# Three late chunk loads of a recurrent-attention and MoE kernel issued in other forms

## The chip, the cores and the metric

The kernel runs on one core of one Trainium2 chip. The metric is the device time of one execution in microseconds (us). TensorE is called PE here, its weight loads PEld, VectorE DVE, ScalarE ACT, GpSimd POOL, SyncE SP. SP does no arithmetic: it issues DMA transfers. A "granted clock" of 1.00 means TensorE ran at full speed.

## The reference: what is computed

Two layers follow each other. The first is a recurrent attention (RWKV-6) over 4 batch rows, 8 heads, 768 positions and 48 values per head. Cut to what matters:

```python
for t in range(S):
    cur = einsum('bhd,bhe->bhde', u[None] * kt, vt)
    y[:, :, t] = einsum('bhd,bhde->bhe', rt, state + cur)
    state = wt[:, :, :, None] * state + einsum('bhd,bhe->bhde', kt, vt)
```

The second takes the result as 3072 tokens of 384 values through two matrix products with a leaky ReLU between them:

```python
h = x @ w_in                      # 384 -> 2048
g = np.maximum(0.01 * h, h)
return (g @ w_out)                # 2048 -> 384
```

Inputs `r`, `k`, `v`, `w` are `(4, 8, 768, 48)` float32 in DRAM, so one head's 128 positions are 24 KB that lie in one piece, and the eight heads lie 147 KB apart.

## The kernel before, in words

The 3072 tokens are cut into 24 chunks of 128 positions. `seq` says which batch row and which part of it chunk `n` is; the chunks interleave the batch rows. The first four chunks go through `pair`, two at a time, the others through `single(n)`. Each chunk of `single` has four loads (`w`, `k`, `r`, `v`, 192 KB each, line 708): 128 partitions by 8 heads by 48 floats, that is 1024 rows of 192 bytes into one buffer of the pool `in`, which holds the four parts side by side. A row of heads fills 1536 bytes of a partition without a gap.

From the loads, `single` makes these steps:

- ACT takes the logarithm of `w` (line 718), PE sums it along the positions (line 724), DVE adds (line 736), ACT takes exponentials (lines 750 and 754), DVE multiplies them with `r` and `k` into `rk` (helper line 407).
- `rk` is transposed into `rkT`: by PE for some chunks, by a DMA transpose from SP for the chunks in `RK_DMA` (line 771). PE forms the scores from `rkT` (line 864), DVE masks them into `m` (line 795).
- POOL multiplies `k` by `u` into `ru` (line 437) and that by `r` (line 441); DVE sums it per head into `dg` (line 445); POOL multiplies `v` by `dg` into `vs` (line 449), and casts `v` to bf16 into `vb` (line 457). POOL also scales the state into `sb` (line 782).
- PE makes `y` from `m`, `vb` and `sb` (lines 831 and 836), DVE adds `vs` (line 482), and `y` is transposed into `xT`, by PE (line 468) or by a DMA transpose from SP (line 849).

The second layer runs in blocks of one or two chunks: products with `w_in_b` (line 1030), leaky ReLU on ACT (line 1045), and, for the late blocks, products with `w_out_b` by a scheme of seven products (line 960) with sums on DVE (lines 941, 974, 981) and ACT (line 976). Line 1013 stores the result.

The order of all steps is written out by hand in `ORDER`, a list of 1123 step numbers, and each engine runs its own steps in that order and never passes one that waits. `Plan` keeps costs too, from which it picks a free buffer of a pool and places warm-up products at the start. The step numbers and `ORDER` are the same before and after the change.

Each DMA signals its landing on one of eight semaphores, `DMAHW0` to `DMAHW7`, which are handed out in turn. A DMA is issued only when the one before it on the same semaphore, eight places earlier, has landed. So at most eight DMAs are under way.

The change touches the function `load` in `single`, for the chunks 20, 21 and 22 of 0 to 23, whose buffers are `in6`, `in4` and `in8`. Chunks 20 and 21 run together (20 is in `MERGED`).

Of the kernel before, what the change touches and what calls it, by code (L numbers as in the profile page):

```python
# [7 lines left out]
F32 = mybir.dt.float32  # L8
# [159 lines left out]
def kernel(  # L168
# [11 lines left out]
    nc = tc.nc  # L180
    B, H, S, D = r.shape
    L = 128
# [36 lines left out]
    pool = ctx.enter_context(tc.tile_pool(name="pool", bufs=1))  # L219
# [3 lines left out]
    def make(name, count, shape, dtype, where=None):  # L223
        pools[name] = [(where or pool).tile(shape, dtype, name=f"{name}{i}") for i in range(count)]
# [12 lines left out]
    w_in_b = pool.tile([128, KT, FF], BF16, name="w_in_b")  # L237
    w_out_b = pool.tile([128, NJ, DM], BF16, name="w_out_b")

    make("in", 11, [128, 1536], F32)  # L240
    make("lw", 3, [128, H, 64], BF16)
    make("lw2", 1, [128, 2, H, 64], BF16)
# [17 lines left out]
    with tc.manual_schedule():  # L260
# [10 lines left out]
        for t in pools["lw"]:  # L271
# [3 lines left out]
            out=trev[:], in_=trev[:], compare_op=ALU.is_ge, fill=0.0,  # L275
# [5 lines left out]
            out=tstr2[:], in_=tstr2[:], compare_op=ALU.is_gt, fill=0.0,  # L281
# [4 lines left out]
            out=ident[:], in_=ident[:], compare_op=ALU.is_equal, fill=0.0,  # L286
# [3 lines left out]
            out=maskb[:], in_=maskb[:], compare_op=ALU.is_gt, fill=0.0,  # L290
            base=0, pattern=[[1, 128]], channel_multiplier=-1,
        )
        for tile_, op in ((mask2, ALU.is_gt), (spread, ALU.is_equal)):
            for q in (0, 64):
                nc.gpsimd.affine_select(
                    out=tile_[q : q + 64, :, :], in_=tile_[q : q + 64, :, :], compare_op=op, fill=0.0,
# [58 lines left out]
        def columns(n):  # L355
            xb, off = place[n]
            return lambda: xb.t[:, :, off : off + L]
# [23 lines left out]
        for part in (1, 2):  # L381
            def rest(e, part=part):
# [8 lines left out]
                out=u_rows.t[0:1, :], in_=u_row.t[0:1, :]),  # L391
# [302 lines left out]
        def single(n):  # L694
            b, c = seq[n]
            t0 = c * L
# [5 lines left out]
            def part(i):  # L702
                return lambda: slot.t[:, i * DM : (i + 1) * DM].rearrange("p (h d) -> p h d", h=H)

            lds = []
            for i, src in enumerate((w, k, r, v)):
                def load(e, src=src, i=i):
                    nc.sync.dma_start(out=part(i)(), in_=src[b, :, t0 : t0 + L, :].rearrange("h p d -> p h d"))
                lds.append(step(
                    {"SP": 0.62}, load, P0 + i * 0.1, takes=[slot], wire=LOAD,  # L710
                    deps=[firsts[n - AHEAD]] if n - AHEAD in firsts else []))
            wl, kl, rl, vl = lds
            wv, kv, rv, vv = (part(i) for i in range(4))

            lw = Buf("lw")
            s_ln = lns[n] = step(
# [24 lines left out]
            for half in range(0 if first else 2):  # L741
# [4 lines left out]
                        out=a_in.t[q0 : q0 + 64, :, half], in_=cp.t[q0 : q0 + 64, DM : DM + NP], func=AF.Exp),  # L746
# [21 lines left out]
            else:  # L768
# [3 lines left out]
                        out=rkT.t[:], in_=rk.t[:].rearrange("p a h d -> p (a h d)")),  # L772
# [4 lines left out]
            if not first:  # L777
# [5 lines left out]
                        out=sb.t[:].rearrange("p g a d -> p (g a) d"),  # L783
# [12 lines left out]
                    out=m.t[:, par, :, :], in0=sc[par].t[:].rearrange("p (g t) -> p g t", g=NP),  # L796
# [49 lines left out]
            else:  # L846
# [3 lines left out]
                        out=columns(n)(), in_=y.t[:].rearrange("p h d -> p (h d)")),  # L850
# [4 lines left out]
        def run(ns):  # L855
            works = [single(n) for n in ns]
            asked = [next(x) for x in works]

            def scores(e):
                for sc, rkT, _ in asked:  # L860
                    for p in range(NP):
                        for par in range(2):
                            q0 = 64 * par
                            nc.tensor.matmul(  # L864
                                sc[par].t[:, p * 128 : (p + 1) * 128], lhsT=rkT.t[q0 : q0 + D, NP + p, :],
                                rhs=rkT.t[q0 : q0 + D, p, :], start=True, stop=True, skip_group_check=True)

            s_sc = step(
                {"PE": 0.19 + 0.231 * len(ns)}, scores, ns[-1] * 10 + 1, deps=[s for x in asked for s in x[2]],
                reads=[x[1] for x in asked], takes=[b for x in asked for b in x[0]])  # L870
            given.append(s_sc)
            for x in works:
                next(x, None)
# [142 lines left out]
        for nb, size in enumerate(blocks):  # L1016
# [7 lines left out]
            for j in range(0, NJ, J):  # L1024
# [15 lines left out]
                if j == 0:  # L1040
                    for ch in chs:
# [4 lines left out]
                        out=g.t[:, j : j + J, 0:N],  # L1046
                        in_=hp.t[:, 0 : J * N].rearrange("p (a n) -> p a n", a=J), func=AF.Prelu, alpha=0.01),
# [86 lines left out]
```

## Time and profile before

| | |
|---|---|
| time, median of 3 runs | 179.33 us (179.13 to 180.84) |
| span of the profiled execution | 177.0 us |
| what lies around the span, against the median | 2.3 us |
| granted clock from 100 us to 160 us | 1.00 |
| PE busy | 170.4 us, 96% |
| DVE busy | 143.5 us, 81% |
| ACT busy | 114.0 us, 64% |
| POOL busy | 107.3 us, 61% |
| chunk loads from line 708 | 80, of 192 KB, 4.1 to 4.7 us from issue to landing |

The profiled execution has no time of its own beside its span, so the span stands for it: the difference to the median, 2.3 us, is taken as what every execution has before and after it. Rows of the timeline give the start (us from the span's start), the duration (us), the engine, the line, the operation, the tiles as out<-in, and how many instructions are merged in the row; a bracket tells how long the engine had been idle before and what ended that. A queue's row (SPq) is the time that the issuing of a DMA took, not its transfer. An answer about one line gives durations as minimum, median and maximum, and the time from issue to landing in the same way.

### The profile page before, as it was taken

Reading aid. Unit: us, or ns where it says so; the run is one execution under the profiler, and the core shown is the slowest. Engines: PE = TensorE matmul, PEld = TensorE weight load, DVE = VectorE, ACT = ScalarE, POOL = GpSimd, SP = SyncE. Lnnn points to the kernel's source line nnn. Section 1 sums busy time; section 2 is a strip of 40 time slices with the busy share of each in tenths; the row PEclk is TensorE's granted clock in tenths of the full one; section 3 lists DMA queues with packets and bytes.
Section 4 is the critical chain, followed back from the end, with each engine's and each line's share of the span. In section 5 each row is a group of like instructions: output and inputs, shape, how many; then the busy total and the mean of one; then the engine's idle time right before and its main releaser. Section 6 shows DMA issues by size and latency. Waiting matters only on the chain.

```text
span 177.0 us, 5530 instructions
## 1 busy us (share of the span) xinstructions
PE 170.4 (96%) x2155; PEld 139.9 (79%) x2158; DVE 143.5 (81%) x299; ACT 114.0 (64%) x263; POOL 107.3 (61%) x143
## 2 busy tenths in 40 slices
PE   7999999999999999999999999999999998999993
PEld 2566779867768877777779899899899997799992
DVE  7498935267599899889879999999999999956662
ACT  5676769734677794796379964676769950178500
POOL 5989946486749859879599093391693959100000
PEclk9999999999999999999999999999999999999999
DMA  5999999999999999999999999996999897432104
GB/s 138 261 271 340 350 300 195 351 231 199 201 206 195 191 199 227 163 201 179 198 206 195 197 208 209 163 222 124 210 194 196 188 226 78 118 101 80 44 26 157
DMA packets 115885, 34.25 MB, mean 194 GB/s; under 512 B 108305, under 2 KB 115090, under 8 KB 115858
## 3 DMA queue, kind: packets, MB, share of 16 engines
q1 hardware_dynamic: 115856, 33.89, 93.1%
q8 instruction: 17, 0.28, 0.7%
q14 instruction: 10, 0.08, 0.2%
q10 hardware_dynamic: 2, 0.00, 0.0%
HBM read 25.17 MB, written 4.72 MB: 169 GB/s over the span
## 4 chain that ended last, share of the span: by engine, by line
PE 69%; DVE 15%; ACT 5%; issue 4%; DMA 3%; POOL 2%; DVEq 0%; SPq 0%; ACTq 0%
PE ps L1030 30%; PE ps L1060 13%; PE ps L960 10%; DVE rk L407 3%; DMA rkT<-rk 3%; PE ps L864 3%; DVE in L941 2%; PE ps L418 2%; ACT g L425 2%; PE ps L724 1%; PE ps L836 1%; DVE ci L736 1%; PE ps L518 1%; DVE dg L445 1%; ACT ps L750 1%
## 5 line engine op out<-in xcount | busy, mean ns | idle before, releaser
L1030 PE MATMUL ps<-xT,w_in_b 128*128 128x256 bf16 (+1 forms) x672 | 70.8, 258 | 0.3 <-DVE rk L407 0.2
L1045 ACT ACTIVATE g<-ps 128x512 bf16<-128x512 f32 x96 | 54.4, 598 | 18.1 <-PE ps L1030 16.0
L1030 PEld LDWEIGHTS <-w_in_b 128*128 128x128 bf16 x672 | 56.9, 98 | 7.8 <-issue 0.6
L437 POOL TENSOR_TENSOR ru<-in,ub 128x384 f32<-128x384 f32 x24 | 24.3, 1017 | 13.1 <-DMA in<-in_k_dram 7.0
L1060 PE MATMUL ps<-w_out_b,g 128*128 128x384 bf16 x160 | 31.4, 326 | 0.0
L407 DVE TENSOR_TENSOR rk<-in,ps 128x384 bf16<-128x384 f32 x48 | 24.8, 547 | 6.1 <-ACT ps L754 2.3
L782 POOL TENSOR_TENSOR sb<-s,a 128x384 bf16<-128x384 f32 x18 | 15.6, 875 | 16.6 <-ACT a L745 8.1
L795 DVE TENSOR_TENSOR m<-ps,maskb 128x512 bf16<-128x512 f32 x40 | 25.1, 682 | 0.3 <-PE ps L864 0.2
L441 POOL TENSOR_TENSOR ru<-ru,in 128x384 f32<-128x384 f32 x24 | 23.8, 1000 | 2.1 <-DMA in<-in_r_dram 1.1
L1060 PEld LDWEIGHTS <-g 128*128 128x128 bf16 x160 | 14.1, 97 | 6.8
L449 POOL TENSOR_TENSOR vs<-in,dg 128x384 f32<-128x384 f32 x20 | 17.4, 874 | 3.0 <-DMA in<-in_v_dram 2.1
L960 PEld LDWEIGHTS <-g 128*128 128x128 bf16 x224 | 18.3, 98 | 0.2
L976 ACT COPY o<-ps 128x192 f32<-128x192 f32 x18 | 5.8, 320 | 17.5 <-PE ps L960 15.5
L960 PEld LDWEIGHTS <-in 128*128 128x128 bf16 x168 | 13.6, 98 | 1.9 <-DVE in L941 1.4
L445 DVE TENSOR_REDUCE dg<-ru 128x8 f32<-128x384 f32 x24 | 12.9, 545 | 1.9 <-POOL ru L441 1.7
L457 POOL CAST vb<-in 128x384 bf16<-128x384 f32 x24 | 12.7, 534 | 2.2 <-DMA in<-in_v_dram 2.2
L981 DVE TENSOR_TENSOR o<-ps,o 128x192 f32<-128x192 f32 x35 | 11.6, 351 | 1.9 <-ACT o L976 1.1
L482 DVE TENSOR_TENSOR y<-ps,vs 128x384 bf16<-128x384 f32 x20 | 10.9, 553 | 2.4 <-PE ps L836 2.3
L754 ACT ACTIVATE ps<-ci 128x384 f32<-128x384 f32 x20 | 9.8, 493 | 4.7 <-DVE ci L736 4.1
L718 ACT ACTIVATE lw<-in 128x384 bf16<-128x384 f32 x20 | 9.9, 521 | 4.1 <-DMA in<-in_w_dram 4.1
L736 DVE TENSOR_TENSOR ci<-ps,lw 128x384 f32<-128x384 f32 x20 | 10.9, 551 | 1.8 <-PE ps L724 1.1
L960 PE MATMUL ps<-in,in 128*128 128x192 bf16 x112 | 11.4, 247 | 0.5 <-DVE in L941 0.5
(105 smaller groups left out, 258.8 us busy)
## 6 DMA issues: line engine op xcount, KB each, us to landing
out_dram<-o SPq DMA_DIRECT2D x23, 192.0 KB, 2.8
in<-in_w_dram SPq DMA_DIRECT2D x20, 192.0 KB, 4.7
in<-in_k_dram SPq DMA_DIRECT2D x20, 192.0 KB, 4.2
in<-in_r_dram SPq DMA_DIRECT2D x20, 192.0 KB, 4.2
in<-in_v_dram SPq DMA_DIRECT2D x20, 192.0 KB, 4.1
in<-in_moe_w_out_dram SPq DMA_DIRECT2D x4, 768.0 KB, 6.9
in<-in_moe_w_in_dram SPq DMA_DIRECT2D x2, 768.0 KB, 9.7
in<-in_moe_w_in_dram SPq DMA_DIRECT2D x4, 384.0 KB, 8.1
```

The costliest lines, as they stand in the source:

```text
L407: (nc.gpsimd if e == "POOL" else nc.vector).tensor_tensor(out=o, in0=x, in1=i, op=ALU.mult)
L437: lambda e: nc.gpsimd.tensor_tensor(out=ru.t[:], in0=kv(), in1=ubv, op=ALU.mult),
L441: lambda e: nc.gpsimd.tensor_tensor(out=ru.t[:], in0=ru.t[:], in1=rv(), op=ALU.mult),
L445: lambda e: nc.vector.tensor_reduce(out=dg.t[:], in_=ru.t[:], axis=AX.X, op=ALU.add),
L449: lambda e: nc.gpsimd.tensor_tensor(out=vs.t[:], in0=vv(), in1=dg.t[:].unsqueeze(2).to_broadcast([128, H, D]), op=ALU.mult),
L457: {"POOL": 0.56}, lambda e: nc.gpsimd.tensor_copy(out=vb.t[:], in_=vv()),
L782: lambda e: nc.gpsimd.tensor_tensor(out=sb.t[:].rearrange("p g a d -> p (g a) d"), in0=s_in.t[:].rearrange("p g a d -> p (g a) d"), in1=a_ ...
L795: lambda e, par=par: nc.vector.tensor_tensor(out=m.t[:, par, :, :], in0=sc[par].t[:].rearrange("p (g t) -> p g t", g=NP), in1=maskb[:].uns ...
L960: nc.tensor.matmul(o(), lhsT=x()[:, i, :], rhs=y()[:, i, :], start=fresh, stop=(stop and i == ii[-1]), skip_group_check=True)
L1030: nc.tensor.matmul(hp.t[:, a * N : (a + 1) * N], lhsT=w_in_b[:, t, (j + a) * 128 : (j + a + 1) * 128], rhs=xb.t[:, t, 0:N], start=(a == 0 ...
L1045: lambda e, hp=hp, g=g, j=j, J=J, N=N: nc.scalar.activation(out=g.t[:, j : j + J, 0:N], in_=hp.t[:, 0 : J * N].rearrange("p (a n) -> p a n ...
L1060: nc.tensor.matmul(op.t[:, 0:DM], lhsT=g.t[:, j, off : off + 128], rhs=w_out_b[:, j, :], start=(j == 0), stop=(j == NJ - 1))
```

## The change

For chunk 20 the loads of `w` and `k` are each issued as eight transfers, one per head, of 128 rows of 192 bytes. For chunk 21 the load of `w` goes into a buffer of its own, `spaced`, in which the heads lie 64 floats (256 bytes) apart, and the logarithm reads it from there. For chunk 22 the load of `v` is issued by ACT instead of SP. The bytes that are moved are the same.

```diff
+    spaced = pool.tile([128, H, 64], F32, name="spaced")
     make("in", 11, [128, 1536], F32)
...
                 def load(e, src=src, i=i):
-                    nc.sync.dma_start(out=part(i)(), in_=src[b, :, t0 : t0 + L, :].rearrange("h p d -> p h d"))
+                    if n == 20 and i < 2:
+                        for h in range(H):
+                            nc.sync.dma_start(out=part(i)()[:, h], in_=src[b, h, t0 : t0 + L, :])
+                    elif n == 21 and i == 0:
+                        nc.sync.dma_start(
+                            out=spaced[:, :, 0:D], in_=src[b, :, t0 : t0 + L, :].rearrange("h p d -> p h d"))
+                    else:
+                        (nc.scalar if n == 22 and i == 3 else nc.sync).dma_start(
+                            out=part(i)(), in_=src[b, :, t0 : t0 + L, :].rearrange("h p d -> p h d"))
...
             wv, kv, rv, vv = (part(i) for i in range(4))
+            if n == 21:
+                wv = lambda: spaced[:, :, 0:D]
```

In the built program the lines shift: the loads of line 708 stand in lines 711 (per head), 713 (spaced) and 716 (all others), 771 becomes 782, 849 becomes 860, 1013 becomes 1024, 437 becomes 438, 441 becomes 442. Names carry a number for the buffer and a second one that is one higher after the change, since `spaced` came in as number 74.

**SP's queue, late in the program.** Before the change, from chunk 21's load of `w` to chunk 20's load of `r`:

```order
L708 DMA in4_78<-in_w_dram 128x8x48
L708 DMA in6_80<-in_w_dram 128x8x48
L1013 DMA out_0_dram<-o2_148 128x384
L849 DMA_TRANSPOSE xT4_144<-y0_132 128x3x128
L849 DMA_TRANSPOSE xT4_144<-y1_133 128x3x128
L771 DMA_TRANSPOSE rkT2_99<-rk3_95 128x8x128
L771 DMA_TRANSPOSE rkT3_100<-rk2_94 128x8x128
L708 DMA in6_80<-in_k_dram 128x8x48
L708 DMA in6_80<-in_r_dram 128x8x48
```

After it, at the same place ("x8" are eight rows in a run):

```order
L713 DMA spaced_74<-in_w_dram 128x8x48
L711 DMA in6_81<-in_w_dram 128x48 x8
L1024 DMA out_0_dram<-o2_149 128x384
L860 DMA_TRANSPOSE xT4_145<-y0_133 128x3x128
L860 DMA_TRANSPOSE xT4_145<-y1_134 128x3x128
L782 DMA_TRANSPOSE rkT2_100<-rk3_96 128x8x128
L782 DMA_TRANSPOSE rkT3_101<-rk2_95 128x8x128
L711 DMA in6_81<-in_k_dram 128x48 x8
L716 DMA in6_81<-in_r_dram 128x8x48
```

The order is the same; two rows became sixteen. The first group after the change, with the semaphores that each row waits for:

```order
L713 DMA spaced_74<-in_w_dram 128x8x48 [waits DMAHW3_49]
L711 DMA in6_81<-in_w_dram 128x48 [waits DMAHW4_49]
L711 DMA in6_81<-in_w_dram 128x48 [waits DMAHW5_49]
L711 DMA in6_81<-in_w_dram 128x48 [waits DMAHW6_49]
L711 DMA in6_81<-in_w_dram 128x48 [waits DMAHW7_49]
L711 DMA in6_81<-in_w_dram 128x48 [waits DMAHW0_49]
L711 DMA in6_81<-in_w_dram 128x48 [waits DMAHW1_49]
L711 DMA in6_81<-in_w_dram 128x48 [waits DMAHW2_49]
L711 DMA in6_81<-in_w_dram 128x48 [waits DMAHW3_49]
L1024 DMA out_0_dram<-o2_149 128x384 [waits DMAHW4_49,DVE_49]
```

The eighth head's transfer waits for `DMAHW3`, on which chunk 21's `w` (the first row) was issued.

**POOL, where chunk 20's `k` and `r` are used.** Before:

```order
L782 TENSOR_TENSOR sb1_129<-s1_123,a1_120 128x384 [waits DVE_49,Activation_49]
L437 TENSOR_TENSOR ru0_107<-in6_80,ub_70 128x384 [waits DMAHW2_49,Pool_49]
L441 TENSOR_TENSOR ru0_107<-ru0_107,in6_80 128x384 [waits DMAHW3_49,Pool_49]
L457 CAST vb1_102<-in10_84 128x384 [waits DMAHW4_49]
L449 TENSOR_TENSOR vs2_114<-in10_84,dg0_109 128x384 [waits DVE_49]
```

After:

```order
L793 TENSOR_TENSOR sb1_130<-s1_124,a1_121 128x384 [waits DVE_49,Activation_49]
L438 TENSOR_TENSOR ru0_108<-in6_81,ub_70 128x384 [waits DMAHW4_49,DMAHW3_49,DMAHW5_49,DMAHW2_49,DMAHW6_49,DMAHW1_49,DMAHW7_49,DMAHW0_49,Pool_49]
L442 TENSOR_TENSOR ru0_108<-ru0_108,in6_81 128x384 [waits DMAHW1_49,Pool_49]
L458 CAST vb1_103<-in10_85 128x384 [waits DMAHW2_49]
L450 TENSOR_TENSOR vs2_115<-in10_85,dg0_110 128x384 [waits DVE_49]
```

The order is the same; the first use of `k` waits for all eight of its transfers.

**ACT, where chunk 22's `v` is issued.** Before, in the run of `COPY`s of line 976:

```order
L976 COPY o1_147<-ps1_152 128x192 [waits PE_49]
L754 ACTIVATE ps4_155<-ci1_90 128x384
L976 COPY o2_148<-ps0_151 128x192 [waits DMAHW6_49,PE_49]
L976 COPY o4_150<-ps1_152 128x192 [waits DMAHW5_49,DMAHW1_49,PE_49]
L976 COPY o2_148<-ps0_151 128x192 [waits PE_49]
```

After:

```order
L987 COPY o1_148<-ps1_153 128x192 [waits PE_49]
L765 ACTIVATE ps4_156<-ci1_91 128x384
L987 COPY o2_149<-ps0_152 128x192 [waits DMAHW4_49,PE_49]
L987 COPY o4_151<-ps1_153 128x192 [waits DMAHW7_49,DMAHW3_49,PE_49]
L716 DMA in8_83<-in_v_dram 128x8x48 [waits DMAHW5_49]
L987 COPY o2_149<-ps0_152 128x192 [waits PE_49]
```

One row came in between the third and the last `COPY` shown; on SP the row of this load is gone.

## The prediction

> **What bounds the kernel now.** I read the page's busy shares and the chain of work that ended last, then the busy time in stretches of 10 us around the change.
>
> ```profile
> PE 170.4 (96%) x2155; PEld 139.9 (79%) x2158; DVE 143.5 (81%) x299; ACT 114.0 (64%) x263; POOL 107.3 (61%) x143
> PE 69%; DVE 15%; ACT 5%; issue 4%; DMA 3%; POOL 2%; DVEq 0%; SPq 0%; ACTq 0%
> 110.00:120.00 10.00, 9.94 (x134) 8.82 (x132) 9.52 (x21) 7.35 (x21) 5.39 (x7) 1.00 0.97 185
> 120.00:130.00 10.00, 10.00 (x129) 9.15 (x127) 9.56 (x20) 6.27 (x15) 5.29 (x7) 1.00 0.95 184
> 130.00:140.00 10.00, 10.00 (x129) 9.11 (x127) 9.82 (x21) 9.02 (x26) 6.95 (x8) 1.00 1.03 186
> 140.00:150.00 10.00, 9.82 (x141) 8.88 (x139) 9.97 (x18) 3.87 (x11) 8.12 (x12) 1.00 0.97 165
> ```
>
> The columns of the last four rows are the stretch, its length, the busy time of PE, PEld, DVE, ACT and POOL, the granted clock, the share of the DMA engines and GB/s. Where the changed loads are issued and used (114 to 150 us), PE is busy all the time, DVE is busy 9.5 to 10 of 10 us, and the DMA engines are at 0.95 to 1.03. Nothing there has room: a stall that reaches DVE or PE has no idle time in which it could be made good. The chain goes from PE to DVE at about 127 us and through chunk 20's `dg`:
>
> ```profile
> 129.47 0.47 DVE ci L736
> 129.94 0.47 DVE dg L445
> ```
>
> **The change part by part.** SP's queue, where two loads become sixteen, is full as well:
>
> ```profile
> 114.50 1.82 SPq L708 DMA_DIRECT2D in<-in_w_dram  x2
> 116.41 0.98 SPq L1013 DMA_DIRECT2D out_dram<-o  x1
> 117.50 2.48 SPq L849 DMA_TRANSPOSE xT<-y  x2
> 120.08 3.05 SPq L771 DMA_TRANSPOSE rkT<-rk  x2
> 123.23 0.53 SPq L708 DMA_DIRECT2D in<-in_k_dram  x1
> 123.85 0.59 SPq L708 DMA_DIRECT2D in<-in_r_dram  x1
> 124.49 0.88 SPq L708 DMA_DIRECT2D in<-in_v_dram  x1
> 126.07 0.36 SPq L1013 DMA_DIRECT2D out_dram<-o  x1
> 126.48 0.43 SPq L708 DMA_DIRECT2D in<-in_k_dram  x1
> 126.96 1.76 SPq L708 DMA_DIRECT2D in<-in_r_dram  x2
> ```
>
> The second of the first row is chunk 20's `w`, the fifth row its `k`, the sixth its `r`. Issuing a 192 KB load takes 0.43 us where the transfers ahead have drained, 0.9 us where they have not.
>
> *The price of one small transfer.* The trace has no load of 128 rows. The nearest row by the number of rows is the store, which also has 128:
>
> ```profile
> L1013 SPq DMA_DIRECT2D out_dram<-o x6: 332/332/335, 163.7 to 174.4; - x6
> DMA to landing us min/median/max: 1.6/1.9/1.9
> ```
>
> The stores of 96 KB and 192 KB among these cost the same 0.33 us, so issuing seems to cost per transfer and not per byte. From above it is bounded by the load of 1024 rows in a queue at work, 0.59 us; from below by an eighth of the drained load, 0.43 / 8 = 0.05 us. I take 0.33 us, as its row has the same number of rows, and 0.05 us between two issues (126.48 + 0.43 to 126.96): 0.38 us each, 3.04 us for eight.
>
> *First group, chunk 20's `w`.* Three answers about single loads, at 114.5 us (chunk 21's `w`), 115.4 us (chunk 20's `w`) and 123.2 us (chunk 20's `k`), each with its time to landing below it:
>
> ```profile
> L708 SPq DMA_DIRECT2D in<-in_w_dram x1: 909/909/909, 114.5 to 114.5; - x1
> DMA to landing us min/median/max: 4.2/4.2/4.2
> ...
> L708 SPq DMA_DIRECT2D in<-in_w_dram x1: 864/864/864, 115.4 to 115.4; - x1
> DMA to landing us min/median/max: 3.9/3.9/3.9
> ...
> L708 SPq DMA_DIRECT2D in<-in_k_dram x1: 532/532/532, 123.2 to 123.2; - x1
> DMA to landing us min/median/max: 3.3/3.3/3.3
> ```
>
> Eight issues from 115.4 us would put the eighth at 115.4 + 7 x 0.38 = 118.1. But it waits on the semaphore of chunk 21's `w`, which lands at 114.5 + 4.2 = 118.7. It ends at 119.1, where the single load ended at 116.3: SP is 2.8 us late. The logarithm that needs this `w` runs only at 124.05 us, and the last head should land by about 122 (118.7 plus at most the 3.3 us of a whole load in a drained queue), so it costs nothing there.
>
> SP makes up a part, as the transfers ahead drain while it issues small ones. The store falls from 0.98 to 0.36 us, the two `rkT` transposes from 3.05 to about 2.6 us (the free one at 147.51 takes 1.24 us); the two `xT` transposes already run at their 1.2 us. That is 1.1 us back, so chunk 20's `k` starts 1.7 us late, at 124.9.
>
> ```profile
> 147.51 1.24 SPq L771 DMA_TRANSPOSE rkT<-rk  x1
> L1030 PEld LDWEIGHTS <-w_in_b x23: 97/98/98, 122.6 to 125.0; 128*128 128x128 bf16 x23
> L849 SPq DMA_TRANSPOSE xT<-y x2: 1186/1196/1206, 117.5 to 118.8; - x2
> DMA to landing us min/median/max: 2.8/3.1/3.5
> ```
>
> What is moved with it: the second `xT` transpose is issued at about 121.0 instead of 118.8 and lands 2.8 us later at 123.8, but PE takes its block up at 122.6. So PE stalls about 1.2 us there. This stall runs beside the one on POOL that follows and is the shorter, so it is not added.
>
> *Second group, chunk 20's `k`.* Eight issues take 3.04 us instead of 0.62 us (123.23 to 123.85), so `r` starts 1.7 + 2.4 = 4.1 us late, at 127.95. It finds a drained queue and lands after 3.3 us, as `k` did, at 131.3. Who waits:
>
> ```profile
> 127.03 1.00 POOL L437 TENSOR_TENSOR ru<-in,ub 128x384 f32<-128x384 f32 x1
> 128.11 1.00 POOL L441 TENSOR_TENSOR ru<-ru,in 128x384 f32<-128x384 f32 x1
> ...
> 136.05 1.41 POOL L437 TENSOR_TENSOR ru<-in,ub 128x384 f32<-128x384 f32 x1 [2.89 <-DMA in<-in_k_dram]
> 129.86 0.54 DVE L445 TENSOR_REDUCE dg<-ru 128x8 f32<-128x384 f32 x1
> 130.32 0.70 DVE L981 TENSOR_TENSOR o<-ps,o 128x192 f32<-128x192 f32 x2
> ```
>
> POOL's product with `k` (127.03) waits for the last head, issued at about 127.6 and landed after 1.9 to 3.3 us, at the latest at 130.9; the product with `r` (128.11) then starts at 131.3 and ends at 132.3. DVE's sum `dg`, which started at 129.86, starts at 132.35: **2.5 us late**. DVE runs in order, so the sums of line 981, the `y` that PE transposes and `rk` all queue behind it. Up to 150 us DVE has 0.2 us of idle time, so the 2.5 us reach the end. The idle 2.89 us that POOL had before chunk 22's `k` would swallow the delay on POOL, but not on DVE.
>
> *Chunk 21's spaced `w`.* Same rows, same count; the logarithm takes it more than 5 us after its landing at 118.7. I cost it at nothing; its price lies between the cheapest and the dearest load row of this stretch (0.43 and 0.98 us of queue), and it would show as part of the first group's 2.8 us. [...]
>
> *Chunk 22's `v` on ACT.*
>
> ```profile
> 144.50 0.32 ACT L976 COPY o<-ps 128x192 f32<-128x192 f32 x1 [0.25 <-PE ps L960]
> 145.16 0.32 ACT L976 COPY o<-ps 128x192 f32<-128x192 f32 x1 [0.34 <-PE ps L960]
> 151.25 0.32 ACT L976 COPY o<-ps 128x192 f32<-128x192 f32 x1 [5.77 <-PE ps L960]
> 144.75 0.57 SPq L708 DMA_DIRECT2D in<-in_v_dram  x1
> ```
>
> It is issued behind the `COPY` of 144.50, so at about 144.85, as SP did at 144.75, and moves with the 2.5 us like all else. Behind it on ACT are one `COPY`, held up by up to 0.3 us, and then 5.77 us of idle time that cover the rest. SP's next issue is the transpose at 147.51, which waits for DVE, so the 0.57 us freed there buy nothing. I take nothing for both; without the cover it would be 0.6 us.
>
> **Sum.** Span 177.0 + 2.5 = 179.5 us; with the 2.3 us around it 181.8 us, against the median 179.33.
>
> [...]
>
> **The rivals.**
>
> *Not slower: issuing costs by the row, not by the transfer.* Take 0.05 us for 128 rows, 0.1 us with the gap. The eighth head of `w` still waits for 118.7, so SP is 2.5 us late (118.8 against 116.3) and, with 1.1 us made up, 1.4 us. Eight heads of `k` take 0.8 instead of 0.62 us; `r` is 1.6 us late at 125.45, lands at 128.75, POOL's product ends at 129.8, and `dg` starts at 129.86 as before. What is left is PE's wait: the second `xT` is issued at 120.65 and lands at 123.45, 0.85 us after PE wants it: 180.2 us, within 1%. The case decides up to about 0.11 us for an issue with its gap, above which `dg` waits. For it speaks that a load with eight times the rows costs 0.43 us and not 2.7; against it that the store of 128 rows costs 0.33 us and not 0.05. [...] Here POOL, ACT and DVE each wait for all eight heads, and landings that came sooner could gain little, as PE is full.
>
> *Dearer: 0.59 us an issue, as for loads in a queue at work.* With 0.64 us each, the first group ends at 120.5 (4.2 late, 3.1 after making up 1.1), the second adds 4.5; `r` is issued at 131.45 and lands at 134.75, and `dg` is 5.9 us late: 185.2 us. For it speaks that the queue holds 0.53 to 0.9 us an issue around here; against it that those are issues with 192 KB in front of each.
>
> **How the numbers follow.** Forecast 0.62, with its own range 180.7 to 183.2 us: an issue of 0.30 to 0.42 us moves `r` by 0.03 x 8 up to 0.09 x 8 us in the second group and about as much, less the waiting for 118.7, in the first, and a landing of 3.1 to 3.7 us moves it by -0.2 to 0.4. Dearer 0.18, not slower 0.20. The range of 179.9 to 184.2 us leaves out half of each of these two. A change of 1%, 1.8 us, is about what a measurement of this kernel can tell from none. Slower by over 1%: 0.48 of the forecast and all of dearer, 0.66. Faster by over 1%: 0.04, out of not slower. Within 1%: 0.30, the lower end of the forecast and the rest of not slower.
>
> **What would show it.** Sixteen issues of line 711 at about 0.33 us; the eighth starting when chunk 21's `w` lands; `r` of chunk 20 issued about 4 us late; POOL's line 442 idle on that DMA; DVE's `dg` starting near 132.3; after it all rows 2.5 us late and no new wait near the end. The prediction is wrong if line 711 costs far from 0.33 us, if the waits for landings among eight small transfers hold SP, if PE's wait for `xT` adds to the one on DVE, or if POOL's wait for `v` at 148 us grows beyond the shift.

## The result, and the profile after

| | median | executions | ratio to before |
|---|---|---|---|
| before | 179.23 us | 179.09 to 180.84 | |
| changed | 188.07 us | 186.44 to 188.44 | 1.0445 (1.0393 to 1.0497) |

Medians are over all executions; the ratios, and the table by clock further down, leave out those that lie over 1.5% above the fastest of their kernel. The change made the kernel 8.8 us slower; the prediction said 2.5. The profiled execution of the changed kernel took 187.72 us with a span of 186.0 us. Its busy shares, from the page:

```profile
PE 171.8 (92%) x2158; PEld 140.6 (76%) x2158; DVE 144.7 (78%) x299; ACT 114.0 (61%) x263; POOL 107.6 (58%) x143
```

PE does as much as before, within 1.4 us, but in a longer span: what was added is waiting. SP's own queue around the change (start, length, line, operation):

```profile
115.33 1.15 SPq L713 DMA_DIRECT2D spaced<-in_w_dram  x1
116.53 4.31 SPq L711 DMA_DIRECT2D in<-in_w_dram  x8
120.94 1.19 SPq L1024 DMA_DIRECT2D out_dram<-o  x1
122.23 2.48 SPq L860 DMA_TRANSPOSE xT<-y  x2
124.81 2.62 SPq L782 DMA_TRANSPOSE rkT<-rk  x2
127.53 3.86 SPq L711 DMA_DIRECT2D in<-in_k_dram  x8
131.49 0.38 SPq L716 DMA_DIRECT2D in<-in_r_dram  x1
```

The same instructions as in the prediction's SP rows, later and later: the spaced load starts 0.8 us behind the packed one of before, the first group of heads ends at 120.84 instead of 116.3 us, `xT` goes at 122.23 instead of 117.50, the second group at 127.53 instead of 123.23, and `r` at 131.49 instead of 123.85 us, 7.6 us late. The instructions of line 711 by their durations (min/median/max in ns), then the time from issue to landing of chunk 20's `r` and of the two `xT` transposes, from answers about single instructions:

```profile
L711 SPq DMA_DIRECT2D in<-in_w_dram x8: 430/431/987, 116.5 to 120.4; - x8
L711 SPq DMA_DIRECT2D in<-in_k_dram x8: 423/430/531, 127.5 to 131.0; - x8
...
L716 SPq DMA_DIRECT2D in<-in_r_dram x1: 378/378/378, 131.5 to 131.5; - x1
DMA to landing us min/median/max: 3.9/3.9/3.9
...
L860 SPq DMA_TRANSPOSE xT<-y x2: 1183/1194/1206, 122.2 to 123.5; - x2
DMA to landing us min/median/max: 2.3/2.3/2.3
```

One small transfer holds SP 0.43 us, not 0.33, and 0.475 us with the gap to the next; eight of them take 3.86 and 4.31 us, as the first of a group is dearer (0.53 and 0.99 us). The second `xT` lands at 123.5 + 2.3 = 125.8 us, `r` at 135.4 us. Who waits for them, from the timeline of PE, POOL and DVE (in brackets the idle time before the instruction and what ended it):

```profile
125.95 2.78 PE L1041 MATMUL ps<-xT,w_in_b 128*128 128x256 bf16 x24 [2.61 <-DMA xT<-y]
134.07 0.82 PE L971 MATMUL ps<-in,g 128*128 128x192 bf16 x8
137.99 0.34 PE L842 MATMUL ps<-sb,rkT 128*128 128x96 bf16 x4 [3.10 <-DVE o L992]
...
134.76 0.99 POOL L438 TENSOR_TENSOR ru<-in,ub 128x384 f32<-128x384 f32 x1 [7.20 <-DMA in<-in_k_dram]
135.83 0.99 POOL L442 TENSOR_TENSOR ru<-ru,in 128x384 f32<-128x384 f32 x1
...
136.85 0.55 DVE L446 TENSOR_REDUCE dg<-ru 128x8 f32<-128x384 f32 x1 [3.67 <-POOL ru L442]
```

The chain that was forecast is there: late `k` and `r`, POOL, DVE's `dg` (7.0 us late), PE. One link differs: POOL waits 7.2 us for `k`'s heads in line 438, and line 442 has no wait for `r`, which landed at 135.4 us, before that line's start at 135.83. At 125.95 us PE is 3.2 us late (0.5 of it was there at 114 us, before any changed load was issued), at 137.99 us 6.5. The end is 9.0 us late (186.0 against 177.0), and what the rest is shows in the busy time by stretches of one us, whose column behind POOL's is the granted clock:

```profile
137.00:138.00 1.00, 0.01 (x1) 0.01 (x1) 1.00 (x4) 0.30 (x2) 1.00 (x2) 1.00 1.10 212
138.00:139.00 1.00, 1.00 (x16) 0.85 (x17) 0.87 (x3) 0.79 (x4) 1.00 (x2) 0.73 1.05 182
139.00:140.00 1.00, 1.00 (x6) 0.67 (x6) 0.97 (x3) 0.47 (x1) 0.92 (x2) 0.50 1.28 217
140.00:141.00 1.00, 1.00 (x9) 0.90 (x8) 1.00 (x3) 0.61 (x2) 0.87 (x2) 0.50 1.29 183
141.00:142.00 1.00, 1.00 (x8) 0.91 (x7) 0.13 (x1) 0.37 (x2) 0.00 (x0) 0.56 1.33 195
```

PE idles from 134.9 to 138.0 us. Half a microsecond after it has started again the clock is halved, for 0.27 / 0.5 + 1 + 1 + 0.44 / 0.5 = 3.4 us, which costs 1.7 us of matmuls: PE is 8.2 us late at 141.75 us. The last 0.8 us are lost behind it, up to 149.3 us. No line of the prediction has this.

### The profile page after: what moved, and what is told of

The parts are those of the page before. It is cut to its first block, busy times and chain, and to the rows that moved or that the text cites. A ratio compares the mean times of both kernels' runs of the same rounds, so it can differ in the third digit from the quotient of the medians.

```text
span 186.0 us, 5556 instructions
## 1 busy us (share of the span) xinstructions
PE 171.8 (92%) x2158; PEld 140.6 (76%) x2158; DVE 144.7 (78%) x299; ACT 114.0 (61%) x263; POOL 107.6 (58%) x143
## 5 line engine op out<-in xcount | busy, mean ns | idle before, releaser
L1041 PE MATMUL ps<-xT,w_in_b 128*128 128x256 bf16 (+1 forms) x672 | 71.7, 259 | 3.4 <-DMA xT<-y 2.6
L729 ACT ACTIVATE lw<-in 128x384 bf16<-128x384 f32 x19 | 9.4, 520 | 6.3 <-DMA in<-in_w_dram 6.3
L971 PE MATMUL ps<-in,in 128*128 128x192 bf16 x112 | 12.1, 255 | 0.5 <-DVE in L952 0.5
```

The lines of the kernel that those rows point to most:

```text
L971: nc.tensor.matmul(o(), lhsT=x()[:, i, :], rhs=y()[:, i, :], start=fresh, stop=(stop and i == ii[-1]), skip_group_check=True)
L1041: nc.tensor.matmul(hp.t[:, a * N : (a + 1) * N], lhsT=w_in_b[:, t, (j + a) * 128 : (j + a + 1) * 128], rhs=xb.t[:, t, 0:N], start=(a == 0 ...
```

## The experiments

The theory to be tested: each small transfer holds SP about 0.47 us, whatever it carries; what stands behind on SP (`xT`, `r`) is late by the sum and reaches PE and DVE; and PE, once idle for some 3 us (3.10 in the changed kernel's trace), pays the halved clock on top. The rivals: small transfers land late or wait for one another; the spaced rows or the issue from ACT are to blame.

### Each part alone

Each of these four kernels keeps one part of the change and puts the others back as they were. The first keeps chunk 20's `w` by heads:

```diff
-                    if n == 20 and i < 2:
+                    if n == 20 and i == 0:
...
-                    elif n == 21 and i == 0:
+                    elif n == -1:
...
-                        (nc.scalar if n == 22 and i == 3 else nc.sync).dma_start(
+                        nc.sync.dma_start(
...
-            if n == 21:
+            if n == -1:
```

> Only chunk 20's w goes by heads; k, the spaced w and v are as before. Theory (each small transfer holds SP for about 0.47 us with its gap, as line 711 showed, and everything behind on SP moves by that): SP about 3 to 4.3 us late at the two xT transposes, PE waits 1.5 to 2.9 us for xT, k and r of chunk 20 are issued 3 to 4.3 us late as single loads and dg is at most 2.7 us late; 181 to 182.5 us, +1.7 to +3.1 us, and PE's clock stays above 0.9 as it never idles 3 us. Rival 'the small transfers land slowly and the wait for eight of them is what costs': nothing much, as the logarithm takes w 3 us after its last landing: within 0.5 us of before. Rival 'the loss of 8.8 us came from the k group alone': within 1 us of before.

Measured: 182.18 us, ratio 1.0188 (1.0117 to 1.0260). SP's first group, PE's block, and the two transposes it needs:

```profile
115.94 4.08 SPq L711 DMA_DIRECT2D in<-in_w_dram  x8
...
125.00 2.78 PE L1041 MATMUL ps<-xT,w_in_b 128*128 128x256 bf16 x24 [1.81 <-DVE in L952]
...
L860 SPq DMA_TRANSPOSE xT<-y x2: 1206/1539/1872, 120.6 to 122.5; - x2
DMA to landing us min/median/max: 2.3/2.7/3.0
```

SP is 3.7 us late at the end of the group (120.02 against 116.3), and PE's block starts 2.3 us late. The row names DVE as the releaser, but that is only the semaphore that came last by the profile: in the next run, with `k` alone, the same sum ends at 124.7 us and PE has started this block at 122.8. The second `xT`, at 122.5 + 2.3 = 124.9 us, is what PE waited for. So the first group costs by itself, where the prediction had PE's wait for `xT` hidden behind the second group's. `dg` is 2.3 us late too (132.15 us), as `k` and `r` are issued 3.3 us late; PE and DVE are late by the same, and this run cannot tell which of the two would be enough.

The second keeps chunk 20's `k` by heads; the other lines are as in the first:

```diff
-                    if n == 20 and i < 2:
+                    if n == 20 and i == 1:
```

> Only chunk 20's k goes by heads. Theory (issue time on SP): the group starts on time at 123.3 and holds SP 3.8 instead of 0.6 us, r is issued about 3.1 us late at 127, lands at 130.3, POOL's product ends at 131.3 and dg is 1.5 us late; 180.8 us, +1.5 us, no stall of PE for xT and no drop of the clock. Rival 'what binds is the landing of the eighth head, as small transfers land late whatever the queue': POOL waits for k until about 130.7 or later, dg +2.5 to +4 us, 182 to 183.5 us. Rival 'not additive': if this and the w group alone together give far less than 8.8 us, the rest comes from their meeting: PE idle for 3 us and the clock that fell to 0.57 behind it.

Measured: 183.67 us, 1.0230 (1.0161 to 1.0298). POOL and DVE, then chunk 20's `r`:

```profile
129.12 1.00 POOL L438 TENSOR_TENSOR ru<-in,ub 128x384 f32<-128x384 f32 x1 [1.92 <-DMA in<-in_k_dram]
132.13 0.99 POOL L442 TENSOR_TENSOR ru<-ru,in 128x384 f32<-128x384 f32 x1 [2.02 <-DMA in<-in_r_dram]
...
133.16 0.55 DVE L446 TENSOR_REDUCE dg<-ru 128x8 f32<-128x384 f32 x1 [3.09 <-POOL ru L442]
...
L716 SPq DMA_DIRECT2D in<-in_r_dram x1: 386/386/386, 127.5 to 127.5; - x1
DMA to landing us min/median/max: 4.5/4.5/4.5
```

The last head does not decide here: POOL takes `k` at 129.12 and waits 2.0 us more for `r`, issued 3.6 us late and landed after 4.5 us, not 3.3. That makes `dg` 3.3 us late, against 1.5 expected. The time fits the rival of late landings better than the theory's 180.8, but the load that lands late is the whole one behind the heads. Of its four executions the one with a clock of 1.0 took 181.81 us, the three with 0.991 took 183.6 to 184.0.

The third keeps chunk 21's spaced `w`:

```diff
-                    if n == 20 and i < 2:
+                    if n == -1:
...
-                        (nc.scalar if n == 22 and i == 3 else nc.sync).dma_start(
+                        nc.sync.dma_start(
```

> Only chunk 21's w goes to rows spaced at 256 bytes. Theory: the load costs SP 0.9 to 1.15 us instead of 0.91 and lands at most 0.8 us later, SP is up to 0.3 us late, and nothing waits for it: within 0.5 us of before. Rival 'the spaced load is what made the first group late' (it landed after 5.0 us, before 4.2): SP 0.8 us late at the transposes and PE waits for xT: +0.5 to +1 us. [...]

Measured: 179.83 us, 1.0037 (1.0009 to 1.0065). In an answer about the tile the spaced load takes 0.87 us of queue and lands after 4.5 us; the packed one took 0.91 and 4.2:

```profile
L713 SPq DMA_DIRECT2D spaced<-in_w_dram x1: 872/872/872, 115.0 to 115.0; - x1
```

This load is not quicker for the spacing. Whether the 0.66 us are the load's, a later run asks again.

The fourth kernel has only chunk 22's `v` on ACT:

```diff
-                    if n == 20 and i < 2:
+                    if n == -1:
...
-                    elif n == 21 and i == 0:
+                    elif n == -1:
...
-            if n == 21:
+            if n == -1:
```

> Only chunk 22's v is issued from ACT. Theory: the issue holds ACT about 0.4 us in front of 5.8 us of idle time and frees 0.57 us on SP ahead of a wait: within 0.5 us of before. Rival 'ACT's queue costs': one COPY of line 976 comes 0.4 us late and DVE behind it, +0.3 to +0.5 us; the other way, SP's freed time lets the next rkT transpose go earlier: down to -0.5 us.

Measured: 179.45 us, 1.0006 (0.9975 to 1.0038). Nothing, as forecast.

The two groups alone, in executions without a halved clock, cost 2.2 us (181.3 and 181.4 against 179.15) and 2.6 us (181.8).

### How the cost goes with the number of transfers

Four transfers of two heads in each group in place of eight; this kernel and the next are edits of the kernel before, without the spaced `w` and the issue from ACT:

```diff
+                    if n == 20 and i < 2:
+                        for h in range(0, H, 2):
+                            nc.sync.dma_start(
+                                out=part(i)()[:, h : h + 2],
+                                in_=src[b, h : h + 2, t0 : t0 + L, :].rearrange("h p d -> p h d"))
+                    else:
...
```

> Chunk 20's w and k go by pairs of heads, four transfers each in place of eight; no spaced w, nothing from ACT. Theory (SP pays about 0.47 us for each transfer with its gap, whatever it carries): the w group ends about 1.8 us later than the single load did, the k group takes 1.9 instead of 0.6 us, r of chunk 20 is issued about 2.8 us late, dg is 1.5 to 2.7 us late, PE waits at most 1 us for xT, never idles for 3 us, and the clock stays at 1.0: 180.7 to 182 us. Rival 'SP pays by the row or by the byte': as many rows and bytes as in the whole loads, no change from before. Rival 'the loss belongs to splitting at all': 185 us and more, as with eight.

Measured: 181.42 us, 1.0121 (1.0043 to 1.0200). The issues and `dg`:

```profile
L711 SPq DMA_DIRECT2D in<-in_w_dram x4: 467/467/704, 115.6 to 117.4; - x4
L711 SPq DMA_DIRECT2D in<-in_k_dram x4: 461/470/532, 124.3 to 125.9; - x4
...
131.02 0.55 DVE L446 TENSOR_REDUCE dg<-ru 128x8 f32<-128x384 f32 x1 [0.93 <-POOL ru L442]
```

Twice the rows cost 0.04 us more per issue. Six issues more than before cost 2.25 us, 0.38 us each.

Then the issues without the small loads: whole loads, and behind each seven transfers of one row that nothing reads.

```diff
                     nc.sync.dma_start(out=part(i)(), in_=src[b, :, t0 : t0 + L, :].rearrange("h p d -> p h d"))
+                    if n == 20 and i < 2:
+                        for h in range(1, H):
+                            nc.sync.dma_start(out=spaced[i : i + 1, h, 0:D], in_=src[b, h, t0 : t0 + 1, :])
```

> Chunk 20's w and k are loaded whole as before, and behind each SP issues seven more transfers of one row of 192 bytes, which nothing reads (work added: 14 transfers). It has the sixteen issues of the change and none of its late data. Theory (SP's time for an issue): each of these costs about 0.43 us though it has one row, the w group ends 3.3 us late, r of chunk 20 is issued 6 to 6.6 us late and dg is 5 to 6 us late: 184 to 187 us, the upper end with the clock's drop. Rival 'SP pays by the row': one row costs 0.05 to 0.1 us, at most 0.7 us for each group: within 1 us of before. Rival 'late landings of the small loads': the data comes whole, within 1 us of before.

Measured: 185.19 us, 1.0252 (1.0125 to 1.0378). In its profiled execution the clock is halved from 136.6 us on, so only rows ahead of 134 us are read from it:

```profile
L712 SPq DMA_DIRECT2D spaced<-in_w_dram x7: 223/250/483, 117.2 to 119.7; - x7
L712 SPq DMA_DIRECT2D spaced<-in_k_dram x7: 233/251/480, 127.1 to 129.2; - x7
...
133.69 0.55 DVE L446 TENSOR_REDUCE dg<-ru 128x8 f32<-128x384 f32 x1 [1.54 <-POOL ru L442]
```

One row costs SP 0.25 us, over half of what 128 rows cost: neither the 0.43 us of the theory nor the 0.05 to 0.1 of a price by the row. There are no late small loads here, and `dg` is still 3.8 us late. The issues alone make most of the delay (3.8 us of 5.7 to 7.0 with all the small loads).

### The clock

The changed kernel with products of zeros (which add nothing) ahead of the last matmul before each of PE's two waits, so that PE is never long idle:

```diff
+FILL, fills = {120: 20, 160: 26}, [0]
...
                         for i in ii:
+                            fills[0] += 1
+                            for _ in range(FILL.get(fills[0], 0)):
+                                nc.tensor.matmul(o(), lhsT=zeros[:, 0:128], rhs=zeros[:, 0:HN], start=False,
+                                                 stop=False, skip_group_check=True)
```

> The changed kernel with 46 more products of zeros on PE, which add nothing to the sums: 20 ahead of the last matmul before PE's wait for xT at about 123 us, 26 ahead of the last before its wait at about 135 us, so that PE is idle there for at most about 1.3 us instead of 2.8 and 3.3 us. Theory (the clock fell to 0.57 for 4 us because PE had been idle for 3 us): no stretch below 0.95 of clock, and 1.7 us less than the changed kernel in the runs that dropped once, 3.4 us less in those that dropped twice: 184.5 to 186.5 us. Rival 'the drop costs nothing, as DVE sets the end': 187.5 to 188.5 us with the clock at 1.0. Rival 'the clock falls for another reason (power, time)': the clock falls all the same, 188 us. Rival 'the added work is in the way': over 188.5 us.

Measured: 184.68 us (184.23 to 184.89), 1.0300 (1.0247 to 1.0353), 3.4 us less than the changed kernel, with 46 matmuls more and all four executions at a clock of 1.0. PE's rows around both waits:

```profile
122.62 1.81 PE L974 MATMUL ps<-zeros 128*128 128x192 bf16 x20
125.11 2.78 PE L1046 MATMUL ps<-xT,w_in_b 128*128 128x256 bf16 x24 [0.59 <-DMA xT<-y]
133.81 2.31 PE L974 MATMUL ps<-zeros 128*128 128x192 bf16 x26
136.68 0.34 PE L843 MATMUL ps<-sb,rkT 128*128 128x96 bf16 x4 [0.48 <-DVE o L997]
```

PE still starts its work late, 5.2 us at 136.68 against 131.49; this execution's span ends 6.1 us late and the median is 5.5 us late, so what is lost before stays lost, and no more than 0.9 us is lost behind. Not all of the 3.4 us is the clock's: POOL got `k` at 133.44 us here and at 134.76 in the changed kernel, so 1.3 of the 2.9 us between the two spans were there before the clock fell.

The kernel with both fills, with chunk 21's `w` packed and chunk 22's `v` on SP:

```diff
-                    elif n == 21 and i == 0:
+                    elif n == -1:
...
-                        (nc.scalar if n == 22 and i == 3 else nc.sync).dma_start(
+                        nc.sync.dma_start(
...
-            if n == 21:
+            if n == -1:
```

> Both groups of heads with the 46 products of zeros on PE, but chunk 21's w packed and chunk 22's v from SP, as before. Theory (neither of these two edits costs or brings anything; the 0.66 us that the spaced load alone showed is drift): the same as with them, 184.68 within 0.4 us. Rival 'the spaced rows cost 0.6 us': 184.0 us. Rival 'the issue from ACT helped': 185.2 us or more.

Measured: 184.31 us, 1.0289 (1.0242 to 1.0335). Its clock was 0.998 or more in all six executions. The two edits together differ from nothing by 0.4 us, and the intervals overlap; the 5.4 us are those of the two groups, 14 issues more at 0.38 us each, the same price as with pairs.

Each fill alone, first the one ahead of the second wait, then the one ahead of the first:

```diff
-FILL, fills = {120: 20, 160: 26}, [0]
+FILL, fills = {160: 26}, [0]
```

```diff
-FILL, fills = {120: 20, 160: 26}, [0]
+FILL, fills = {120: 20}, [0]
```

> The changed kernel with only the 26 products of zeros ahead of PE's second wait (about 135 us), which add nothing to the sums. Theory (each of PE's two long waits can cost one drop of the clock, 1.7 us, and the changed kernel's median had both in two of four runs): no drop behind 135 us; a drop behind the first wait at 123 us remains in some runs: 184.7 us without it, 186.4 with it. Rival 'the two fills bring their 3.4 us in another way than through the clock': 186.4 us with the clock at 1.0.

> The changed kernel with only the 20 products of zeros ahead of PE's first wait (about 123 us). Theory: no drop behind the first wait, and the drop behind the second, where PE idles for over 3 us, in every run: mean clock 0.991, 186.2 to 187 us, 1.7 us over the kernel with both fills. Rival 'the drop costs nothing, as DVE sets the end': 184.7 us at a clock of 0.991.

Measured: 185.75 us, 1.0360 (1.0303 to 1.0417), and 186.69 us, 1.0454 (1.0364 to 1.0544). The order of the medians is as expected, but the intervals overlap, and the second ratio lies above what its three shorter executions give (185.85 to 187.13 us, 1.036 to 1.043 of the 179.42 us before). The detail is not as expected. With the first fill alone the profiled execution kept its clock, though PE idled for 2.7 us:

```profile
136.72 0.34 PE L843 MATMUL ps<-sb,rkT 128*128 128x96 bf16 x4 [2.67 <-DVE o L997]
...
138.00:142.00 4.00, 4.00 (x45) 3.56 (x43) 3.93 (x10) 3.55 (x11) 1.63 (x2) 1.00 1.28 182
```

So an idle time of this length may or may not bring the halved clock, and executions of the kernel with the second fill alone that kept a clock of 1.0 took 184.91 and 185.85 us, which the clock does not explain. How the 3.4 us divide between the two waits stays open.

### Which wait ends last

As in the run with `k` alone by heads, but `r` issued ahead of the heads (an edit of the kernel before):

```diff
+                    whole = lambda j, s: nc.sync.dma_start(
+                        out=part(j)(), in_=s[b, :, t0 : t0 + L, :].rearrange("h p d -> p h d"))
+                    if n == 20 and i == 1:
+                        whole(2, r)
+                        for h in range(H):
+                            nc.sync.dma_start(out=part(i)()[:, h], in_=src[b, h, t0 : t0 + L, :])
+                    elif n != 20 or i != 2:
+                        whole(i, src)
```

> Chunk 20's k by heads as in the run with k alone, but its r is issued ahead of the eight heads. SP spends the same time and the heads land 0.6 us later than there; only r comes first. Theory (r, held up behind the heads on SP, is the wait that ends last): r is issued on time and lands at about 127.5, the eighth head is issued at about 127.5 and lands at 129.4 to 129.8, POOL's product with r ends at about 132 without a wait of its own, dg is 1.8 to 2.3 us late instead of 3.3, PE idles under 2 us and the clock stays at 1.0: 180.5 to 181.5 us, some 2.5 us less than with k alone in the usual order, most of it the clock's drop that does not come. Rival 'the total of issues decides, in whatever order' or 'the small loads land late': as with k alone, 183 to 184 us. Rival 'v, now last behind the heads, is the next wait': dg on time as above, but POOL's vs late, DVE's y another 0.5 to 1 us late: 182 us.

Measured: 1.0174 (1.0073 to 1.0275) against 1.0230; the median of 183.28 us is not what was expected. The profile tells the two causes apart:

```profile
41.62 0.32 PE L732 MATMUL ps<-lw,trev 128*128 128x384 bf16 x1 [1.94 <-ACT lw L726]
42.00:46.00 4.00, 4.00 (x24) 2.43 (x21) 2.18 (x5) 2.48 (x6) 2.89 (x4) 0.58 0.87 153
...
132.66 1.00 POOL L442 TENSOR_TENSOR ru<-ru,in 128x384 f32<-128x384 f32 x1
...
133.69 0.55 DVE L446 TENSOR_REDUCE dg<-ru 128x8 f32<-128x384 f32 x1 [1.75 <-POOL ru L442]
```

POOL's product with `r` no longer waits for its load, and `dg` starts 3.8 us late. In this execution the clock was already halved at 42 to 46 us, behind an idle time of 1.94 us and long before the change; from there to the change the rows are about 1.9 us late, so that 1.9 us of the 3.8 are the change's (3.3 before the two were swapped). The mechanism holds for `k` alone, in one trace each. The one execution with a clock of 1.0 took 181.0 us, against 181.8 with `r` behind; the gain of 2.5 us did not come, as the clock fell in the other executions all the same, in the profiled one in a place that the change does not touch.

## Why the prediction was right in direction and wrong in size

**Right: the place and the chain.** SP is the queue that pays; POOL's two products, `dg` and PE follow as forecast, and with both fills the end keeps PE's delay within 0.9 us. PE's wait for `xT` does run beside the one on DVE: PE is 3.2 us late behind the first and 6.5 behind the second, less than the 7.0 of `dg` and not their sum. The spaced load and the issue from ACT cost nothing that can be told.

**Wrong, first: the price of one small transfer.** The step that failed is the 0.33 us taken from the store with the same number of rows. Line 711 costs 0.43 us, 0.475 us with its gap where 0.38 was taken. It was nearer to the quicker whole loads around it (0.38 to 0.53 us) than to the store. The wait of the eighth head for chunk 21's `w` does not decide at this price: with the first group alone the eight follow each other without a gap (0.76 + 7 x 0.47 = 4.1 us).

**Wrong, second: the 1.1 us made up.** The store took 1.19 us in place of 0.36, and of the 4.5 us only 0.2 were made up. With the first group alone the store fell to 0.38 us and the `rkT` pair to 2.63 us as forecast, but the first `xT` rose to 1.87; 0.4 of 3.7 us came back.

**Wrong, third: a landing of 3.3 us, and the wait that ends last.** `r` landed after 3.9 us here and 4.5 us with `k` alone; the last section shows that in the changed kernel the last of sixteen updates came 1.0 us behind the others. The sign that was named, line 442 idle on `r`, came with `k` alone and not in the changed kernel: there `k`'s last head, 3.7 us on its way, held POOL until 134.76 us. The prediction let that head land as late as 130.9 us and still started the product with `r` at 131.3; with the 1.0 us of the product with `k` between them it would have been 131.9.

These give `r`: predicted 4.1 us late at its issue, measured 7.6. The 3.5 us between come from 1.7 at the end of the first group (0.8 of it was there when the spaced load started, which with the fills starts at 114.35 to 114.93 instead of 115.33 us, so it is this execution's and not the change's; 0.2 is that load's own, the rest the dearer issue), 0.9 not made up, and 0.9 in the second group. Put into the prediction's own sum, 0.475 us an issue and nothing made up, the first group ends at 115.4 + 8 x 0.475 = 119.2 us, 2.9 late; `k` starts at 126.1 and `r` at 129.9, lands at 133.2, and `dg` is 4.4 us late: 183.7 us, against medians of 184.3 and 184.7 measured with both fills.

**Wrong, fourth: a term that was missing.** A PE idle of some 3 us was not priced, though the prediction left PE waiting for 2.5 us. With both fills the median is 3.4 us lower (188.07 against 184.68). The trace shows one halved stretch, which costs 1.7 us; two of the four executions have twice the loss of clock (0.982), so an estimate is 2.5 us on the mean of the four, and the rest is of other origin, as the earlier `k` above. By kernel, executions whose mean clock stayed at 0.997 or more against those at 0.988 to 0.991:

| kernel | clock near 1.0 | clock near 0.99 |
|---|---|---|
| before | 178.3 to 180.2 | 180.2, 180.9, 181.1 |
| first group alone | 181.3, 181.4 | 182.9, 183.3 |
| second group alone | 181.8 | 183.6, 183.7, 184.0 |
| one-row issues | 182.5 | 185.1 |
| `r` ahead of the heads | 181.0 | 182.9, 183.6 |
| changed | | 186.4, 187.7 (and two of 188.4 at 0.982) |
| changed, second fill alone | 184.9, 185.9 | 185.7 |
| changed, first fill alone | 185.9 | 186.3, 187.1 |
| changed, both fills | 184.2 to 184.9 | |

The clock of the kernel before falls too, in 5 of 43 executions (three of them in the table), so a halved clock alone does not show the change; that all four executions of the changed kernel had one, and none of the ten of the two kernels with both fills, does.

The rival of dearer issues (185.2 us) came nearest in time, 2.9 us short. That is luck: its 0.59 us an issue is not what line 711 shows, and it stands in for the 1.1 us that were not made up and the later landings.

## What to carry to other kernels

Where SP issues one transfer behind another, each costs its issue, here 0.43 us with 24 KB, 0.47 with 48 KB and 0.38 to 0.53 for the quicker ones of 192 KB, and the bill comes to whatever stands behind it: find out which of those loads is used next, and put it ahead (`dg` 1.9 us late instead of 3.3 with `k` alone). Take the price from the same kind of instruction in the nearest state of the queue, a load from a load, and let no saving into the sum that no row shows. When a wait of some 2 to 3 us lands on a full PE, reckon with a halved clock behind it: 1.7 us in the changed kernel's trace, and in some executions and not in others.

## What the runs showed of the hardware

The clock's half step comes late and had about the same length in all four traces that have one in mid-kernel: 3.4 us in the changed kernel, with `k` alone by heads, with the one-row issues (0.18 / 0.5 + 3 + 0.03 / 0.5 from rows of one us) and with `r` ahead of the heads (0.42 x 4 / 0.5). In the changed kernel it begins 3.6 us after PE's last matmul, 0.5 us into its new work; with `k` alone by heads PE idled for 2.5 us, and the stretch looks alike:

```profile
135.00:136.00 1.00, 0.88 (x6) 0.55 (x4) 0.87 (x3) 0.57 (x2) 0.92 (x2) 0.55 0.92 177
136.00:137.00 1.00, 1.00 (x9) 0.83 (x7) 0.97 (x4) 0.31 (x1) 1.00 (x2) 0.50 1.19 241
137.00:138.00 1.00, 1.00 (x8) 0.92 (x7) 0.44 (x1) 0.66 (x2) 0.18 (x1) 0.50 1.17 190
138.00:139.00 1.00, 1.00 (x9) 0.81 (x8) 0.36 (x2) 0.71 (x2) 0.00 (x0) 0.74 1.24 202
```

0.45 / 0.5 + 1 + 1 + 0.26 / 0.5 = 3.4 us again. The length of the idle time before it does not decide alone: gaps of 1.94 (`r` ahead of the heads), 2.10 (one-row issues), 2.52 (`k` alone) and 3.10 us (changed kernel) were followed by a halved clock, gaps of 1.87 (second fill alone), 2.61 (the first wait of the changed kernel) and 2.67 us (first fill alone) were not, in one trace each.

An issue's price on SP grew little with the size of these transfers: 0.25 us for one row, 0.43 for 128, 0.47 for 256, and from 0.38 to 0.53 for the 1024 rows of the quicker whole loads (0.38 for chunk 20's `r` in the changed kernel, 0.43 at 126.48 us and 0.53 at 123.23 us before); the two at 114.50 and 115.45 us took 0.91 and 0.86 us. That the transfers ahead have drained, as the prediction has it, does not tell these apart by the times of issue and landing in the trace of before: four were under way ahead of the load at 142.01 us (0.38 us), as ahead of the one at 114.50 us (0.91 us), and two ahead of the one at 123.23 us (0.53 us).

Late last updates. In the changed kernel the last head of `k`, issued at 130.96 us, landed after 3.7 us, where the seven others took at most 2.3. The trace has sixteen updates of the semaphore for each landing, and the page counts sixteen DMA engines; that each update is one engine's is not shown. Fifteen of this head's came by 132.96 us, the sixteenth at 134.63. `r` had fifteen by 134.38 and the last at 135.38. Between 131.5 and 133.6 us the trace has one packet of a queue that the profile calls instruction:

```profile
q8 instruction: 1, 0.02, 3.9%
```

3.9% of 16 engines in 2.1 us are 1.3 us of one engine; the packet's own record runs from 132.20 to 133.50 us. The traces of before and of the changed kernel bear it out from 60 to 160 us: of 154 loads, heads and stores 38 (18 and 20) had their sixteenth update over 0.7 us behind the fifteenth, and all 38 had an instruction packet (queue 8 or 14) moving while they were under way, as 48 of those in time had; of the 68 with no such packet, none was late in this way. The kernel before has as many of these packets (17 on queue 8 and 10 on queue 14 on either page), so they are not the change's; what the change does is to put eight small loads, all of which one product waits for, where such a packet falls. No run moved the packets, so this stays a coincidence in time, if a close one. An estimate of its worth here, from the updates above: had the last head and `r` landed with their fifteenth updates, `dg` would have come up to 1.4 us earlier.
